# Attention and two expert layers on one core: third pair's weights in a buffer of their own, first product between the last steps, packed weights' casts ahead of their differences

## The chip, the cores and the metric

The kernel runs on one core of one Trainium2 chip. The metric is the device time of one execution in microseconds (us), as the median over runs. A core has engines that run side by side, each through its own list of instructions in order: TensorE (PE, matrix products), VectorE (DVE), ScalarE (ACT), GpSimd (POOL), and SyncE (SP), which here issues the DMA transfers. An instruction that needs a result of another engine waits at the head of its list, and everything behind it waits too.

## The reference

All arrays are float32. Attention runs twice per batch of 8 and head of 8: 32 packed queries attend to 576 tokens, and the tokens attend to the packed result. Two expert layers follow over 4608 tokens of width 512.

```python
    p_packed = sm_attn(p, k, v)
    out = sm_attn(q, p_packed, p_packed)
...
    h = x @ w_in
    g = np.where(h > 0.0, h, alpha * (np.exp(np.minimum(h, 0.0)) - 1.0))
    return (g @ w_out).astype(np.float32)
...
    a = x @ w_a
    b = x @ w_b
    return (a * b @ w_out).astype(np.float32)
```

`w_in` is 512 x 2048, `w_a` and `w_b` are 512 x 1536.

## The kernel before

A float32 product is made of three products of a shorter type (fp32r): each factor is split into a high word, which ScalarE casts, and a low word, which VectorE gets as a difference (`split`, L81 to L83). So nearly every tile that TensorE reads was first touched by ScalarE, then by VectorE.

**First phase** (to about 801 us). Eight blocks, one per batch, of 32 steps each; a step is a half h of the batch's tokens and a tile f of the hidden width. `l1` (L446) makes the hidden tile h with six matmuls (L455). `act1` (L461) makes the activation: ScalarE relu and exponential (ge, L463 and L464), VectorE gf (L467), ScalarE cast gr (L469), VectorE difference gr (L471). `l2` (L474) makes twelve matmuls into four accumulators x2a (L477), two steps later, through the list `pend`; it reads the cast in its first matmuls and the difference in the others. After the 16 steps of a half `x2_out` (L485) copies the accumulators out (L494 on ScalarE, L495 on VectorE) and stores them to x2d in memory (L496).

Between the steps lie the attention of the next batch and the conversion of the second expert layer's weights. They are put into a list with a time (`put`, L516; two units are a step), and `run_until` (L519) writes them into the program when the steps have come to that time. From block 1 on, TensorE, VectorE and ScalarE run in the order in which the program is written; SyncE's order, and all of block 0, are set by the scheduler. In attention, `wp` (L373) multiplies the packed result by the first layer's weights, one chunk c of four at a time, and `wps` (L378) splits the two rows of banks of such a chunk into the ring buffers wr that `l1` reads. `o_hi` and `o_lo` (L705, L708) split the rows of the last weights and store them to od. `pT` (L107) is a transpose of the packed queries on TensorE, with a copy by VectorE.

**Second phase.** Six groups of tokens; for each, twelve pairs f of weight tiles. `l3` (L878) makes seven products of sums (six matmuls each, L868) in banks A, B and C for a pair, with the sums of weights in a tile e (1792 KB) and the sums of activations s (22 steps, `s_steps`, L797, from the four tiles x2f that `x_load`, L786, brings back from x2d). ScalarE copies A and C (p1, p5), VectorE makes u, v and w of them. `l4` (L910) multiplies the result by wo into the group's accumulators, nine matmuls per pair (L912). The first group's s steps, and the e tiles of pairs 0 and 1, are made or loaded inside block 7 of the first phase. All other e tiles of the first group are loaded by `e_load` (L781, issue L783), into two buffers that pairs share in turn, so a load waits for the pair two before it to be done. The tiles for pairs 9 and 11 (`E_LATER`) are still computed in the first group (`e_words`, L761, brings the raw words wl; `e_step`, L769, works in the one buffer "em"; L680 stores to ed). `o_load` (L856, issue L858) brings wo, twelve loads of 512 KB.

```python
        E_LATER = {9: 1, 11: 5}
...
            put(T7 + 42 + 0.9 * n, s_step, 0, n)
...
                acc = [bank2("acc", f"o{g}_{t}", TT) for t in range(TT)]
                for f in range(NF2):
                    c1[f], c2[f] = l3(g, f)
                    if f + 2 < NF2:
                        e_load(f + 2, g)
```

Of the kernel before, what the change touches and what calls it, by code (L numbers as in the profile page):

```python
# [20 lines left out]
P = 128  # L21
# [4 lines left out]
def program(tc, q, k, v, p, w_in, w_out, w_a, w_b, w_out2, out):  # L26
# [34 lines left out]
    with ctx:  # L61
# [316 lines left out]
        def wps(b, c, r):  # L378
            w = ring_r[st[b, "wp", c]][r]
            split(w[:, 0, :], w[:, 1, :], st[b, "wpp"][r])  # L380
            if r == 1:
                done.add(("wp", b, c))

        def attention(b, tokens=False):

# [5 lines left out]
            def at_times(k, load_q, pt, s1s, sm1, q, sm1bs, at, at5, p, ppt, s2s, wps_):  # L391
# [26 lines left out]
                for c, t in enumerate(wps_):  # L418
                    add(t, wp, c, takes=("wp", b, c))
                    add(t + 1, wps, c, 0)  # L420
                    add(t + 2 if tokens else t + 1, wps, c, 1, frees=("wp", b, c))

# [192 lines left out]
        for b in range(1, B):  # L615
            for t, fn, takes, frees in attention(b):
                late = t > 64
                if b == 1:
                    packed = {48: 58, 49: 59, 52: 62, 53: 63, 56: 66, 57: 67, 60: 73, 61: 74}
                    t = packed.get(t, t + 2.3 if late else 22 + 0.8 * max(t, 0))  # L620
                    late = t > 64
                put(2 * NF * 2 * (b - 1) + t, fn, chain=(b, late), takes=takes, frees=frees)
# [99 lines left out]
        for b in range(1, B - 1):  # L722
            t, f = 4 * NF * b, 2 * (b - 1)
            first = (A1, B1, O1) if f in E_IN_1 else ((11, 12, 15), (18, 19, 21), O1)
            for f_, times in ((f, first), (f + 1, (A2, B2, O2))):
                for kind, x in zip("abo", times):
                    put(t + x[0] - 16, w2_load, kind, f_)
                    for n, y in enumerate((*x, x[2] + 3)):
                        put(t + y, w2_step, kind, f_, n)
            for f_, x, y in ((f, 25, 26), (f + 1, 61, 67)):  # L730
                put(t + x, o_hi, f_)
# [100 lines left out]
        E_IN_7 = (3, 5, 7, 0, 1)  # L832
        E_LATER = {9: 1, 11: 5}
        assert sorted((*E_IN_1, *E_IN_7, *E_LATER)) == list(range(NF2))
# [8 lines left out]
        for n in range(NS):  # L843
            put(T7 + 42 + 0.9 * n, s_step, 0, n)
        m1_block(B - 1)
        while pend:
            run_pend()
        order.close()
        order.enter_context(tc.manual_schedule(engines={ET.PE}))
        ps_stack.close()  # L850
        m1_stack.close()
        p4 = ctx.enter_context(tc.tile_pool(name="p4", bufs=2, side="right", reuse_waits="tile"))
        ps2 = ctx.enter_context(tc.tile_pool(name="ps2", bufs=1, space=PSUM, reuse_waits="tile"))
        wo = {}

        def o_load(f):  # L856
            wo[f] = p4.tile([P, 2, 512], F32R, tag=f"wo{f}", name=f"wo{f}", bufs=1)
            nc.sync.dma_start(wo[f].bitcast(F32), od[f])  # L858

        def bank2(tag, name, bufs):  # L860
# [3 lines left out]
        def product(bank, f, i, first=True):  # L864
            n = 0
            for k in range(2):
                for wi, xi in ((0, 0), (0, 1), (1, 0)):
# [8 lines left out]
                    n += 1  # L876

        def l3(g, f):  # L878
            def tmp(tag):
# [6 lines left out]

            bA, bB, bC = (bank2(x, f"{x}{g}_{f}", n) for x, n in (("A", 2), ("B", 2), ("C", 1)))
            pA, pB, pC = (x[:, :HT] for x in (bA, bB, bC))
            p1, u, v, p5, w = (tmp(x) for x in ("p1", "u", "v", "p5", "w"))
            product(bA, f, 1)  # L890
            nc.scalar.copy(p1, pA)  # L891
# [28 lines left out]
        def out_rows(g, t, acc):  # L920
# [6 lines left out]
            nc.sync.dma_start(out[r0:r0 + P, :], o)  # L927

        with order:
            for g in range(NG):  # L930
                c1, c2 = {}, {}
                acc = [bank2("acc", f"o{g}_{t}", TT) for t in range(TT)]
                for f in range(NF2):
                    c1[f], c2[f] = l3(g, f)
                    if f + 2 < NF2:
                        e_load(f + 2, g)
                    if g == 0:
                        o_load(f)
                        for n, f0 in E_LATER.items():
                            if f == f0 - 1:  # L940
                                e_words(n, True)
                            if 0 <= f - f0 < 3:
                                for names in E_STEPS[2 * (f - f0):2 * (f - f0) + 2]:
                                    for name in names:
                                        e_step(n, name, p4, "em", 1)
                    if f:
                        for t in range(TT):
# [48 lines left out]
```

## Time and profile before

| | before |
|---|---|
| median of 3 runs | 1641.36 us (1640.78 to 1642.24) |
| profiled execution, its own time | 1641.99 us |
| its span | 1640.2 us |
| TensorE, VectorE, ScalarE busy | 96%, 62%, 44% |
| mean granted clock of TensorE | 0.979 of full speed |

The span runs from the first to the last instruction of the one profiled execution; the time has a little more around it. A timeline row gives the start, the duration and the engine, the line of the program, what is written from what (`out<-in`), and how often; in brackets stands the idle time of the engine just before, and what ended it. SPq is SyncE issuing a transfer.

### The profile page before, as it was taken

The page shows a single profiled execution, that of the slowest core. Times are in us where ns is not written, and L with a number is a line of the kernel's source. Part 1 is how long each engine was busy: PE and PEld are TensorE (multiplying, and loading weights), DVE is VectorE, ACT ScalarE, POOL GpSimd, SP SyncE. Part 2 cuts the span into 40 slices and gives each one's busy share as a digit, 9 for nine tenths or more (in the row PEclk, how much of TensorE's full clock was granted, in tenths as well). Part 3 has the DMA queues.
Part 4 walks back from the last instruction along what each step waited for, and adds up shares of the span by engine and source line. Part 5 has one row for each costly group of instructions (what it writes and reads, how often), then busy time and mean ns, then how long its engine had stood idle before and what let it go on. Part 6 is the DMA issues. An engine that isn't in the chain of part 4 may idle for free.

```text
span 1640.2 us, 27529 instructions
## 1 busy us (share of the span) xinstructions
PE 1568.5 (96%) x10824; PEld 1437.7 (88%) x10824; DVE 1024.9 (62%) x2180; ACT 724.4 (44%) x1633; POOL 93.6 (6%) x74
## 2 busy tenths in 40 slices
PE   5498999999999999999899999999999999999998
PEld 3286898989898998989889899999989989998997
DVE  6999576777777777767645544635545454563451
ACT  6576566667676767667422212312222221231221
POOL 3321010100000001000000000000000000000000
PEclk7599999999999999999999999999999999999999
DMA  8755344626272543327495545535545553553541
GB/s 253 186 155 131 106 108 108 170 54 188 69 197 82 147 127 104 112 106 264 177 369 184 202 149 215 212 136 180 203 143 212 192 199 148 194 208 109 202 179 39
DMA packets 215505, 267.34 MB, mean 163 GB/s; under 512 B 150224, under 2 KB 180944, under 8 KB 205520
## 3 DMA queue, kind: packets, MB, share of 16 engines
q1 hardware_dynamic: 215376, 265.59, 48.8%
q8 instruction: 85, 1.39, 0.3%
q14 instruction: 44, 0.36, 0.1%
HBM read 213.52 MB, written 52.04 MB: 162 GB/s over the span
## 4 chain that ended last, share of the span: by engine, by line
PE 73%; DVE 11%; ACT 8%; DMA 4%; issue 2%; SPq 1%; POOL 0%; DVEq 0%; ACTq 0%
PE o L912 18%; PE x2a L477 16%; PE B L868 13%; PE A L868 9%; PE C L868 8%; PE h L455 8%; DVE gf L467 2%; DVE wr L83 2%; ACT gr L469 2%; ACT wr L82 2%; ACT ge L464 1%; DMA wst_i<-in_moe_w_in_dram 1%; ACT ge L463 1%; DVE gr L471 1%; DVE s L83 1%
## 5 line engine op out<-in xcount | busy, mean ns | idle before, releaser
L477 PE MATMUL x2a<-gr,wout 128*128 128x288 f32 x3072 | 464.7, 299 | 7.8 <-DVE x2s L495 2.4
L477 PEld LDWEIGHTS x2a<-gr,wout 128*128 128x128 f32 x3072 | 422.1, 189 | 51.6 <-issue 12.8
L912 PE MATMUL o<-wo,c 128*128 128x512 f32 x1296 | 307.7, 391 | 0.0
L912 PEld LDWEIGHTS o<-wo,c 128*128 128x128 f32 x1296 | 242.5, 188 | 47.8
L455 PE MATMUL h<-a,wr 128*128 128x288 f32 x1536 | 250.8, 299 | 17.0 <-DVE gf L467 9.4
L868 PE MATMUL B<-s,e 128*128 128x384 f32 x1296 | 261.3, 336 | 2.4 <-DVE u L893 1.0
L455 PEld LDWEIGHTS h<-a,wr 128*128 128x128 f32 x1536 | 220.9, 191 | 24.1 <-DVE gf L467 11.7
L868 PEld LDWEIGHTS B<-s,e 128*128 128x128 f32 x1296 | 228.2, 188 | 4.5 <-DVE v L898 2.4
L868 PE MATMUL A<-s,e 128*128 128x384 f32 x864 | 176.0, 338 | 5.5 <-DMA e<-ed 5.5
L868 PE MATMUL C<-s,e 128*128 128x384 f32 x864 | 173.9, 335 | 0.0
L868 PEld LDWEIGHTS A<-s,e 128*128 128x128 f32 x864 | 154.7, 189 | 12.0 <-DMA e<-ed 6.3
L469 ACT CAST gr<-gf 128x288 fp32r<-128x288 f32 x256 | 110.7, 433 | 121.3 <-DVE gf L467 120.1
L868 PEld LDWEIGHTS C<-s,e 128*128 128x128 f32 x864 | 152.7, 189 | 0.0
L82 ACT CAST c<-u 128x384 fp32r<-128x384 f32 x72 | 36.9, 513 | 259.2 <-DVE u L901 259.2
L467 DVE SCALAR_TENSOR_TENSOR gf<-ge,h 128x288 f32<-128x288 f32 x256 | 113.4, 443 | 58.1 <-ACT ge L464 54.7
L898 DVE TENSOR_TENSOR v<-p,B 128x384 f32<-128x384 f32 x72 | 39.8, 553 | 162.8 <-PE B L868 162.8
L471 DVE TENSOR_TENSOR gr<-gf,gr 128x288 fp32r<-128x288 f32 x256 | 124.1, 485 | 20.0 <-ACT gr L469 18.3
L463 ACT ACTIVATE ge<-h 128x288 f32<-128x288 f32 x256 | 104.6, 409 | 58.2 <-PE h L455 57.4
L464 ACT ACTIVATE ge<-ge 128x288 f32<-128x288 f32 x256 | 113.8, 445 | 7.6
L893 DVE TENSOR_TENSOR u<-p,B 128x384 f32<-128x384 f32 x72 | 39.8, 553 | 117.5 <-PE B L868 117.5
L891 ACT COPY p<-A 128x384 f32<-128x384 f32 x72 | 34.7, 482 | 136.7 <-PE A L868 136.7
L895 ACT COPY p<-C 128x384 f32<-128x384 f32 x72 | 34.7, 482 | 109.7 <-PE C L868 109.7
(357 smaller groups left out, 1398.1 us busy)
## 6 DMA issues: line engine op xcount, KB each, us to landing
e<-ed SPq DMA_DIRECT2D x70, 1792.0 KB, 7.2
ed<-e SPq DMA_DIRECT2D x7, 1792.0 KB, 6.7
x2d<-x2s SPq DMA_DIRECT2D x32, 288.0 KB, 2.7
out_dram<-osb SPq DMA_DIRECT2D x36, 256.0 KB, 2.0
v<-in_v_dram SPq DMA_DIRECT2D x8, 1024.0 KB, 6.8
wst_i<-in_moe_w_in_dram SPq DMA_DIRECT2D x16, 512.0 KB, 5.7
wst_o<-in_moe_w_out_dram SPq DMA_DIRECT2D x16, 512.0 KB, 4.9
kst<-in_k_dram SPq DMA_DIRECT2D x112, 72.0 KB, 2.6
```

The source lines that it names most:

```text
L82: nc.scalar.copy(hi, src)
L83: nc.vector.tensor_tensor(lo, src, hi.bitcast(F32), op=ALU.subtract)
L455: nc.tensor.matmul(t[:, :HS], w[:, wi, o * P:(o + 1) * P], x[:, xi, :], start=(n == 0), stop=(n == 5))
L463: nc.scalar.activation(e, t[:, :HS], AF.Relu, scale=-1.0)
L464: nc.scalar.activation(e, e, AF.Exp, scale=-1.0)
L467: nc.vector.scalar_tensor_tensor(g, e, -1.0, t[:, :HS], op0=ALU.add, op1=ALU.max)
L469: nc.scalar.copy(gr[:, 0, :], g)
L471: nc.vector.tensor_tensor(gr[:, 1, :], g, gr[:, 0, :].bitcast(F32), op=ALU.subtract)
L477: nc.tensor.matmul(acc[d][:, :HS], wout_r[f][:, wi, d * P:(d + 1) * P], gr[:, xi, :], start=(first and n == 0), stop=(last and n == 2),)
L868: nc.tensor.matmul(bank[:, :HT], es[f][:, E_OF[i], wi, k * P:(k + 1) * P], ss[i][:, xi, k, :], start=(first and n == 0), stop=(n == 5), sk ...
L893: nc.vector.tensor_tensor(u, p1, pB, op=ALU.add)
L912: nc.tensor.matmul(acc, cr[:, xi, t * P:(t + 1) * P], wo[f][:, wi, :], start=(f == 0 and n == 0), stop=(f == NF2 - 1 and n == 2),)
```

## The change

1. The split of the packed weights (blocks 1 to 7) is written as two functions: `wps_hi` makes both casts, `wps_lo` both differences, the latter one unit of time later than the casts.
2. For batch 1 the table `packed`, which sets the times of wp and its splits in block 0 and the first steps of block 1, gets other times. wp_1 comes ahead of x2a of h_1_8's step, wp_2 directly behind the transpose pTp at the end of block 0, wp_3 one step later than before, behind h_0_5.
3. `o_lo` of the second weight row of a block goes from 67 to 65.
4. `E_LATER` goes from {9: 1, 11: 5} to {9: 3, 11: 6}.
5. The s steps go from 42 + 0.9 n to 40.5 + 0.85 n.
6. The first product A of the second phase, before split in two lots of three matmuls among the steps of block 7, is written with all six between the last two `l2` of the first phase.
7. The e tile of pair 2 gets a buffer of its own ("em", shared with the tiles of pairs 9 and 11 afterwards), and its load is written ahead of the second phase; the loads for pairs 3 and 4 are written one pair earlier.
8. The accumulators of a group are allocated at pair 1 and no more at its start.

```diff
+        def wps_hi(b, c):
+            for r in range(2):
+                nc.scalar.copy(ring_r[st[b, "wp", c]][r][:, 0, :], st[b, "wpp"][r])
+
+        def wps_lo(b, c):
+            for r in range(2):
+                w = ring_r[st[b, "wp", c]][r]
+                nc.vector.tensor_tensor(w[:, 1, :], st[b, "wpp"][r], w[:, 0, :].bitcast(F32), op=ALU.subtract)
+            done.add(("wp", b, c))
...
-                    add(t + 1, wps, c, 0)
-                    add(t + 2 if tokens else t + 1, wps, c, 1, frees=("wp", b, c))
+                    if tokens:
+                        add(t + 1, wps, c, 0)
+                        add(t + 2, wps, c, 1, frees=("wp", b, c))
+                    else:
+                        add(t + 1, wps_hi, c)
+                        add(t + 2, wps_lo, c, frees=("wp", b, c))
...
-                    packed = {48: 58, 49: 59, 52: 62, 53: 63, 56: 66, 57: 67, 60: 73, 61: 74}
+                    packed = {
+                        48: 58, 49: 59, 50: 60, 52: 62, 53: 63, 54: 63.5, 56: 64.5, 57: 65, 58: 66, 60: 74.5, 61: 75, 62: 77
+                    }
...
-            for f_, x, y in ((f, 25, 26), (f + 1, 61, 67)):
+            for f_, x, y in ((f, 25, 26), (f + 1, 61, 65)):
...
-        E_LATER = {9: 1, 11: 5}
+        E_LATER = {9: 3, 11: 6}
...
-            put(T7 + 42 + 0.9 * n, s_step, 0, n)
+            put(T7 + 40.5 + 0.85 * n, s_step, 0, n)
...
-        while pend:
-            run_pend()
+        run_pend()
+        first_a = [bank2("A", "A0_0", 2)]
+        product(first_a[0], 0, 1)
+        run_pend()
+        assert not pend
...
+            started = bool(first_a)
+            bA = first_a.pop() if started else bank2("A", f"A{g}_{f}", 2)
...
+            if not started:
+                product(bA, f, 1)
...
+        es[2] = p4.tile([P, 7, 2, 2 * P], F32R, tag="em", name="e2_0_2", bufs=1)
+        nc.sync.dma_start(es[2].bitcast(F32), ed[2])
...
-                acc = [bank2("acc", f"o{g}_{t}", TT) for t in range(TT)]
...
-                    if f + 2 < NF2:
+                    if f + 2 < NF2 and (g or f > 2):
                         e_load(f + 2, g)
                     if g == 0:
+                        if f < 2:
+                            e_load(f + 3, g)
...
+                    if f == 1:
+                        acc = [bank2("acc", f"o{g}_{t}", TT) for t in range(TT)]
```

**VectorE at the start of a block** (here block 4; blocks 2 to 6 have the same). gf and gr are the activation's steps, wst_2o is the difference of `o_lo`, a the result of attention, x2s the copies of the finished accumulators. Before:

```order
L467 SCALAR_TENSOR_TENSOR gf_0_0_5829<-ge_0_0_5813,h_0_0_5806 128x288
L471 TENSOR_TENSOR gr_0_0_5831<-gf_0_0_5829,gr_0_0_5831 128x288
L467 SCALAR_TENSOR_TENSOR gf_0_1_5856<-ge_0_1_5853,h_0_1_5846 128x288
L367 TENSOR_TENSOR a_4_1_0_5860<-t_5096,a_4_1_0_5860 128x288
L710 TENSOR_TENSOR wst_2o_5359<-wm_2o_5644,wst_2o_5359 128x512
L471 TENSOR_TENSOR gr_0_1_5858<-gf_0_1_5856,gr_0_1_5858 128x288
L495 COPY x2s_1_0_0_5878<-x2a_1_0_1_5325 128x288
L495 COPY x2s_1_2_0_5882<-x2a_1_0_3_5327 128x288
```

With the change:

```order
L481 SCALAR_TENSOR_TENSOR gf_0_0_5829<-ge_0_0_5813,h_0_0_5806 128x288
L726 TENSOR_TENSOR wst_2o_5359<-wm_2o_5644,wst_2o_5359 128x512
L485 TENSOR_TENSOR gr_0_0_5831<-gf_0_0_5829,gr_0_0_5831 128x288
L481 SCALAR_TENSOR_TENSOR gf_0_1_5858<-ge_0_1_5855,h_0_1_5848 128x288
L367 TENSOR_TENSOR a_4_1_0_5862<-t_5096,a_4_1_0_5862 128x288
L485 TENSOR_TENSOR gr_0_1_5860<-gf_0_1_5858,gr_0_1_5860 128x288
L509 COPY x2s_1_0_0_5878<-x2a_1_0_1_5325 128x288
L509 COPY x2s_1_2_0_5882<-x2a_1_0_3_5327 128x288
```

The difference of `o_lo` moved from behind a to ahead of the first step's gr; what follows it up to the two copies stands one place earlier.

**TensorE at the end of the first phase.** A_0 is the first product of the second phase, x2a are the accumulators of the last half, gr_1_14 and gr_1_15 the activations of its last two steps. Before:

```order
L868 MATMUL A_0_10624<-s_0_10247,e_0_9999 128x384 x3
L455 MATMUL h_1_7_10304<-a_7_1_0_9524,wr_0_107 128x288 x3
L455 MATMUL h_1_7_10304<-a_7_1_1_9529,wr_1_108 128x288 x3
L477 MATMUL x2a_1_0_0_10160<-gr_1_5_10258,wout_88 128x288
L868 MATMUL A_0_10624<-s_0_10247,e_0_9999 128x384 x3
...
L477 MATMUL x2a_1_0_3_10163<-gr_1_14_10533,wout_97 128x288 x3
L477 MATMUL x2a_1_0_0_10160<-gr_1_15_10562,wout_98 128x288 x3
...
L477 MATMUL x2a_1_0_3_10163<-gr_1_15_10562,wout_98 128x288 x3
L868 MATMUL B_0_10625<-s_0_10249,e_0_9999 128x384 x6
```

With the change:

```order
L491 MATMUL x2a_1_0_3_10163<-gr_1_14_10535,wout_97 128x288 x3
L869 MATMUL A_0_10589<-s_0_10224,e_0_9999 128x384 x6
L491 MATMUL x2a_1_0_0_10160<-gr_1_15_10562,wout_98 128x288 x3
...
L491 MATMUL x2a_1_0_3_10163<-gr_1_15_10562,wout_98 128x288 x3
L869 MATMUL B_0_10630<-s_0_10226,e_0_9999 128x384 x6
L869 MATMUL C_0_10631<-s_0_10225,e_0_9999 128x384 x6
L869 MATMUL A_0_10589<-s_0_10228,e_0_9999 128x384 x6
```

The product A_0 moved from the steps around h_1_7 to between the products of gr_1_14 and those of gr_1_15.

**SyncE at the border of the phases.** x2d are the last two stores of the first phase; wo, wl and e_0_2 as above; ed_158 is the store of pair 9's computed tile. Before:

```order
L496 DMA x2d_1_124<-x2s_1_0_0_10601 128x576
L496 DMA x2d_1_124<-x2s_1_2_0_10605 128x576
L858 DMA wo_10691<-od_161 128x1024
L766 DMA wl_10693<-wfb_146 128x512
...
L858 DMA wo_11260<-od_168 128x1024
L766 DMA wl_11014<-wfa_136 128x512
L766 DMA wl_11014<-wfb_148 128x512
L858 DMA wo_11342<-od_169 128x1024
L783 DMA e_0_2_10689<-ed_151 128x3584
L858 DMA wo_11420<-od_170 128x1024
...
L680 DMA ed_158<-e_9_10765 128x3584
L783 DMA e_0_3_10761<-ed_152 128x3584
```

With the change:

```order
L510 DMA x2d_1_124<-x2s_1_0_0_10608 128x576
L510 DMA x2d_1_124<-x2s_1_2_0_10612 128x576
L952 DMA e_0_2_10628<-ed_151 128x3584
L895 DMA wo_10690<-od_161 128x1024
...
L895 DMA wo_11420<-od_170 128x1024
L799 DMA e_0_3_10688<-ed_152 128x3584
L895 DMA wo_11496<-od_171 128x1024
L895 DMA wo_11584<-od_172 128x1024
L782 DMA wl_11092<-wfa_136 128x512
L799 DMA e_0_4_10757<-ed_153 128x3584
L782 DMA wl_11092<-wfb_148 128x512
```

The load of e_0_2 moved to directly behind the two stores, e_0_3 and e_0_4 moved ahead of the store of pair 9.

## Rows read from the trace of the kernel before

**Rows 1.** The page, busy time by engine: us, share, instructions.

```profile
PE 1568.5 (96%) x10824; PEld 1437.7 (88%) x10824; DVE 1024.9 (62%) x2180; ACT 724.4 (44%) x1633; POOL 93.6 (6%) x74
```

**Rows 2.** TensorE's waits, 200 to 797 us: total us, times, longest.

```profile
PE x2a L477 <- DVE x2s L495: 2.4, 5, 0.5
PE x2a L477 <- ACT x2s L494: 1.3, 2, 0.9
...
PE x2a L477 <- DVE gr L471: 0.3, 1, 0.3
```

**Rows 3.** The same from 797 us to the end.

```profile
PE A L868 <- DMA e<-ed: 5.5, 1, 5.5
PE B L868 <- DVE u L893: 1.0, 1, 1.0
PE x2a L477 <- DVE gr L471: 1.0, 1, 1.0
```

**Rows 4.** Timelines of TensorE and VectorE, blocks 0 and 1.

```profile
183.56 0.72 PE L242 MATMUL s__2143<-kT,pT 64*32 64x288 f32 x16 [0.95 <-DVE wr L83]
...
199.26 0.92 PE L455 MATMUL h<-a,wr 128*128 128x288 f32 x5 [1.53 <-DVE gf L467]
...
197.49 0.69 DVE L83 TENSOR_TENSOR wr<-wp__2242,wr 128x512 fp32r<-128x512 f32 x1 [0.65 <-ACT wr L82]
```

**Rows 5.** Timelines of VectorE and TensorE, start of block 4.

```profile
452.77 0.46 DVE L471 TENSOR_TENSOR gr<-gf,gr 128x288 fp32r<-128x288 f32 x1 [0.50 <-ACT gr L469]
...
455.22 0.68 DVE L710 TENSOR_TENSOR wst_2o<-wm_2o,wst_2o 128x512 fp32r<-128x512 f32 x1
...
456.19 0.81 DVE L495 COPY x2s<-x2a 128x288 f32<-128x288 f32 x2
...
456.70 1.07 PE L477 MATMUL x2a<-gr,wout 128*128 128x288 f32 x6 [0.48 <-DVE x2s L495]
```

**Rows 6.** Chain of waits, end of the first phase: start, us, what.

```profile
768.55 4.01 DMA x2f<-x2d
...
797.11 0.46 DVE gr L471
...
797.62 3.35 PE x2a L477 x23
```

**Rows 7.** TensorE's timeline, end of the first phase and first pairs.

```profile
772.96 0.68 PE L868 MATMUL A<-s,e 128*128 128x384 f32 x3
...
796.24 0.40 PE L477 MATMUL x2a<-gr,wout 128*128 128x288 f32 x1 [0.36 <-ACT gr L469]
...
801.50 1.31 PE L868 MATMUL B<-s,e 128*128 128x384 f32 x6 [0.55 <-DVE x2s L495]
802.66 1.20 PE L868 MATMUL C<-s,e 128*128 128x384 f32 x6
803.70 1.20 PE L868 MATMUL A<-s,e 128*128 128x384 f32 x6
...
824.17 2.29 PE L868 MATMUL A<-s,e 128*128 128x384 f32 x6 [5.49 <-DMA e<-ed]
...
855.47 1.23 PE L868 MATMUL A<-s,e 128*128 128x384 f32 x6
...
864.87 1.23 PE L868 MATMUL A<-s,e 128*128 128x384 f32 x6
```

**Rows 8.** SyncE's timeline at the border, and the page's DMA issues (KB each, us to landing).

```profile
801.93 0.56 SPq L858 DMA_DIRECT2D wo<-od  x1
...
e<-ed SPq DMA_DIRECT2D x70, 1792.0 KB, 7.2
```

**Rows 9.** Table by stretch: busy us per engine, granted clock, DMA share, GB/s.

```profile
802.00:808.00 6.00, 6.00 (x36) 6.00 (x35) 1.75 (x4) 0.53 (x2) 0.00 (x0) 1.00 0.92 300
...
824.00:830.00 6.00, 5.83 (x18) 5.83 (x19) 0.56 (x1) 0.48 (x1) 0.00 (x0) 0.50 1.04 431
...
840.00:850.00 10.00, 10.00 (x56) 9.60 (x56) 6.52 (x13) 2.47 (x5) 0.00 (x0) 1.00 1.01 417
```

More of the change, by code (lines that the diff above doesn't have):

```diff
@@ L843, in program @@
         for n in range(NS):
-            put(T7 + 42 + 0.9 * n, s_step, 0, n)
-        m1_block(B - 1)
-        while pend:
-            run_pend()
[L848 to L858, printed above, removed]
+            put(T7 + 40.5 + 0.85 * n, s_step, 0, n)
         def bank2(tag, name, bufs):
@@ L876, in product, with o_load @@
                     n += 1
+        m1_block(B - 1)
+        run_pend()
[3 more added lines that the diff above has]
+        assert not pend
+        order.close()
+        order.enter_context(tc.manual_schedule(engines={ET.PE}))
+        ps_stack.close()
+        m1_stack.close()
+        p4 = ctx.enter_context(tc.tile_pool(name="p4", bufs=2, side="right", reuse_waits="tile"))
+        ps2 = ctx.enter_context(tc.tile_pool(name="ps2", bufs=1, space=PSUM, reuse_waits="tile"))
+        wo = {}
+        def o_load(f):
+            wo[f] = p4.tile([P, 2, 512], F32R, tag=f"wo{f}", name=f"wo{f}", bufs=1)
+            nc.sync.dma_start(wo[f].bitcast(F32), od[f])
         def l3(g, f):
@@ L885, in halves @@
                 return r
-            bA, bB, bC = (bank2(x, f"{x}{g}_{f}", n) for x, n in (("A", 2), ("B", 2), ("C", 1)))
+            started = bool(first_a)
+            bA = first_a.pop() if started else bank2("A", f"A{g}_{f}", 2)
+            bB, bC = (bank2(x, f"{x}{g}_{f}", n) for x, n in (("B", 2), ("C", 1)))
             pA, pB, pC = (x[:, :HT] for x in (bA, bB, bC))
             p1, u, v, p5, w = (tmp(x) for x in ("p1", "u", "v", "p5", "w"))
-            product(bA, f, 1)
+            if not started:
+                product(bA, f, 1)
             nc.scalar.copy(p1, pA)
```

## The prediction

> **What bounds the kernel now.** I read the page's busy times first: TensorE is busy 96% of the span [rows 1], so only TensorE's own waits can be won back, and work of other engines counts only where TensorE stands for it. The list of TensorE's waits comes next, in two stretches. From 200 to 797 us, in the first phase, five waits for a VectorE copy of a finished accumulator make 2.4 us, two for a ScalarE copy 1.3, one for a difference 0.3 [rows 2]. From 797 us on, one wait for the weights of a pair is 5.5 us and two of 1.0 stand beside it [rows 3]. The timelines then show what the waited-for engine did just before [rows 4, 5]; the chain of waits shows what held the end of the first phase [rows 6]; TensorE's and SyncE's timelines and the table by stretch show the border [rows 7 to 9]. The sum is made against the profiled execution, 1641.99 us (span 1640.2), 0.63 above the median of 1641.36; I take its difference over to the median.
>
> I call t0 the end of the first phase's last x2a product: 797.62 + 3.35 = 800.97 in the kernel before [rows 6].
>
> **Blocks 0 and 1.** TensorE waits 0.95 us for the second difference of wp_2 ahead of s, and 1.53 us for a gf that stands behind the differences of wp_3 [rows 4]. VectorE itself waits 0.65 between the two wp_3 differences, for ScalarE's next cast: that is the alternation which casts first, differences later, removes. wp_3 now goes behind gf_0_6, and wp_2 right behind the transpose pTp, whose copy it must then wait for. Nothing is removed from VectorE, so between -1.53 and 0 for the first I take -1.0 (the wait's cause, the two differences, leaves that gf's place whole, but lands ahead of gr_0_6), and between -0.95 and +0.5 for the second -0.5. wp_1's earlier place I cost at nothing: TensorE there waits for VectorE anyway. **-1.5** (bounds -2.5 to +0.5).
>
> **Five block boundaries.** Each boundary of blocks 1 to 6 has VectorE idle 0.50 us ahead of gr_0_0, and one step later a difference of o_lo (0.68) ahead of gr_0_1 and the two copies that TensorE waits for, 0.48 us [rows 5]. The o_lo difference goes into the idle place: gr_0_0 is 0.2 late, covered by the lag of two steps between gr and its x2a; the copies come 0.6 earlier, more than the 0.48. Its store to od and the load of pn pass each other on SyncE; od is read in the second phase only. 5 x 0.48 = **-2.4** (bounds -2.4 to 0). **Block 6 to 7**: the waits of 0.3 and 0.9 [rows 2] follow the alternation of wp_3's casts and differences. Now both differences stand behind gr_1_14, and o_lo leaves the block's first steps. I take the 0.3 and a third of the 0.9: **-0.6** (bounds -1.2 to 0).
>
> **End of the first phase.** The s steps cannot begin before x2f lands at 772.56; from there ScalarE and VectorE alternate, step after step, up to the difference of gr_1_14 at 797.11 [rows 6]. Starting the steps earlier in the order moves none of the 22 ahead of that landing in time worth naming, so the difference of gr_1_14 stays near 797.57. The first product's six matmuls stood at 772.96 and 1.5 us later, 0.68 each in two lots, with no wait ahead [rows 7]; there they only used time in which TensorE runs ahead of ScalarE and VectorE. Behind gr_1_14 they cost their 1.04 (six matmuls at the products' spacing) unless they fill a wait. The waits in question are 0.36 and 0.98 [rows 7, 3]; the s steps now end two activation steps before the end, so some of them goes: I take a third of the 1.34. t0 moves by +1.04 - 0.44 = **+0.6** (bounds -0.3 and +1.04).
>
> **After t0.** Before, the third pair's weights e_0_2 were issued behind nine wo and three wl, and landed as A_2 started, 824.17, after 5.49 of idle; the clock was at 0.50, that is 1.2 GHz, from 824 to 830, so six us of work at half speed cost some 2.9 more [rows 7 to 9]. Now e_0_2 is issued where the first wo was, 801.93, and a load of e lands 7.2 later [rows 8]: 809.1, t0 + 8.2. It is needed at t0 + 16.2: from B at 801.50 to A at 824.17 are 22.67, less the waits of 5.49 and 0.99 [rows 7, 3]. So that wait goes, with the half clock; the 0.55 ahead of B goes too, as B and C no longer take the banks that the x2s copies still read. I take u's 0.99 as gone, since VectorE has no s steps left to finish.
>
> But the queue carries all else as before, at 417 GB/s when full [rows 9]. Sizes are from the order's shapes at 4 bytes: 1.835 MB for e or a store to ed, 0.524 for wo, 0.262 for wl, 1.573 for the eight x2f. Behind e_0_2 stand ten wo, one wl, then e_0_3: 7.34 MB, 17.6 us, landing at 826.7, t0 + 25.8. Pairs are 9.4 apart (855.47 to 864.87 [rows 7]), so A_3 is due at t0 + 25.6: a wait of 0.2. From there to e_0_6 stand two wo, two wl, e_0_4, ed_9, e_0_5, x2f, ed_11 and e_0_6: 12.32 MB, 29.5 us, landing at t0 + 55.3, while A_6 is due at t0 + 54.0: **a new wait of some 1.3 us at the seventh pair**. e_0_4 and e_0_5 come in time. A_6 then starts at t0 + 55.3 instead of 864.87 - 800.97 = 63.9: **-8.6** (bounds -10.1 with no wait, -7 with 1.6 us more in the queue's start or a drop of clock behind the new wait). The steps of e_9 and e_11, later now, lie on ScalarE and VectorE; their results are first read for the tenth and twelfth pairs, 45 us after the stores. From A_6 on nothing differs.
>
> On that rate a page differs: the Trainium skill, DMA: Bandwidth & Descriptors, section "Where 436 GB/s comes from", holds that loads from HBM bind at some 358 GB/s per core. The trace shows 417 over ten us [rows 9], so the measurement decides; by 358 the sum would come to -4.0 in place of -12.5.
>
> **Sum**: -1.5 - 2.4 - 0.6 + 0.6 - 8.6 = **-12.5 us**: the profiled execution 1629.5, the median **1628.9**.
>
> **Rivals.**
> (a) *All waits go.* The queue keeps up and A_6 starts at t0 + 53.8 (-10.1); t0 moves by -0.3, blocks 0 and 1 give -2.5, block 6 to 7 -1.2, the boundaries -2.4: -16.5, 1624.9. For it: 1.3 us is little against 55; against: the count of bytes, and VectorE's load in block 0.
> (b) *The queue is slower.* Between 802 and 808, with the queue not yet full, it moved 300 GB/s [rows 9]. From 801.93 to e_0_6 there are 21.5 MB behind 2.8 us of start-up. At 358 GB/s, midway between 300 and 417, e_0_6 lands at t0 + 63.8, and only -4.0 is left: 1637.4; at 380, 1633.9. For it: e_0_2 now leads, and SyncE issues with gaps; against: 431 and 417 in the later stretches [rows 9]. The rule of the Trainium skill's DMA page, above, would bring this case.
> (c) *The early load is not early.* The buffer of its own shares memory with the first phase's tiles; if its load still waits until the first pair is done (six products, t0 + 6.2), e_0_2 is in time, but all that SyncE holds behind it comes 5.3 later: A_6 at t0 + 60.6, -3.3, sum -7.2: 1634.2. For it: the pool opens over released memory; against: those weights were last read long before t0.
> (d) *Slower.* The same queue, if the 300 GB/s of its first six us lasted up to e_0_6: 71.7 us for the bytes, A_6 at t0 + 75.4, +11.5, sum +7.6: 1649.0. With the other terms at -3.9 the change loses below 336 GB/s, and by over 0.2% below 319. Neither later stretch is near that.
>
> **How the numbers follow.** What a measurement of this kernel can tell from no change is some 0.2%, 3.3 us. The forecast has 0.55 (1626.5 to 1632), (a) 0.18, (b) 0.12, (c) 0.08, (d) 0.03, and 0.04 that two terms of the first phase turn into losses and little is left. The range 1624.5 to 1635.5 takes in (a), (c) and (b) down to 370 GB/s; left out are the rest of (b), (d), the 0.04 and a little below (a). Faster than 1638.1: all but (d) and most of the last, 0.92; the same 0.05; slower 0.03.
>
> **What would show it.** In the waits: the five for the x2s copies gone, gf's 1.53 gone, no wait for e at A_2 and a clock of 1.00 from t0 on; a short wait for e at A_3, and one of 1 to 2 us at A_6; x2a still waiting near 797, t0 within a us of 801.6. Wrong would be: a wait at A_2; a wait over 3 us at A_3 (then (b) or (c), told apart by when e_0_2 is issued); half clock behind a new wait; a new wait at pT or gr_0_6 in block 1 as long as those removed; t0 later than 802.

## The result and the profile after

| | before | after |
|---|---|---|
| median of 3 runs | 1641.36 us | 1626.11 us (1625.30 to 1629.78) |
| ratio, 95% interval | | 0.9912 (0.9888 to 0.9937) |
| timed again, median | 1644.00 us (7 runs) | 1629.74 us (4 runs), 0.9914 (0.9899 to 0.9929) |
| profiled execution, its own time | 1641.99 us | 1629.78 us |
| its span | 1640.2 us | 1628.0 us |
| forecast | | 1628.9 us (1624.5 to 1635.5) |

The kernel is faster by some 15 us (0.9%) in the first timing and 14 in the second; the forecast was 12.5. Sum and sign were right. The parts were not: two gains were far too small, two too large, one loss too small, and they nearly cancelled. That the sum came out is luck.

TensorE's waits in the profile after, from 150 to 200 us, from 200 to 797 and from 797 on (three lists; total us, times, longest). Hold them beside [rows 2, 3, 4]:

```profile
PE wp__1930 L242 <- DVE t L340: 2.4, 1, 2.4
PE x2a L491 <- DVE gr L485: 0.5, 1, 0.5
PE wp__2066 L242 <- DVE pT L111: 0.4, 1, 0.4
...
PE aTp L283 <- DVE wr L391: 2.8, 1, 2.8
PE x2a L491 <- DVE gr L485: 1.9, 5, 0.5
PE x2a L491 <- ACT x2s L508: 0.4, 1, 0.4
...
PE A L869 <- DMA e<-ed: 3.0, 2, 2.2
PE B L869 <- DVE v L920: 0.9, 5, 0.2
```

A_n is the first product of pair n in the first group. Gone are the five waits for VectorE's x2s copies, gf's 1.53, the 0.95 ahead of s, u's 0.99 and the 5.49 ahead of A_2. New are 2.8 us of a transpose aTp in block 1, 0.4 of wp for the copy pT, five waits for a difference gr in the second half of block 7, and two for the e tiles of later pairs.

TensorE's timeline after, end of the first phase and the first pairs, to hold beside [rows 7]:

```profile
786.64 1.75 PE L491 MATMUL x2a<-gr,wout 128*128 128x288 f32 x11 [0.47 <-DVE gr L485]
...
789.66 3.31 PE L491 MATMUL x2a<-gr,wout 128*128 128x288 f32 x23 [0.35 <-DVE gr L485]
792.81 1.21 PE L869 MATMUL A<-s,e 128*128 128x384 f32 x6
793.85 1.76 PE L491 MATMUL x2a<-gr,wout 128*128 128x288 f32 x12
795.45 1.21 PE L869 MATMUL B<-s,e 128*128 128x384 f32 x6
...
811.07 1.21 PE L869 MATMUL A<-s,e 128*128 128x384 f32 x6
...
822.75 1.31 PE L869 MATMUL A<-s,e 128*128 128x384 f32 x6 [2.16 <-DMA e<-ed]
...
852.48 1.34 PE L869 MATMUL A<-s,e 128*128 128x384 f32 x6 [0.86 <-DMA e<-ed]
```

B starts behind the last x2a without a wait, A_2 (811.07) behind the first o products without one, A_3 waits 2.16 and A_6 0.86. A_0 stands whole at 792.81, and TensorE had work on both sides of it: no idle time is shown behind 789.66.

To see where the time went I cut each profiled execution at the same products in TensorE's timeline: the first h of block 2, of block 7 and of block 7's second half (its 17th step), the first B behind the last x2a, and A_8, behind which the first group runs without waits. Lengths in us:

| profile | start to block 2 | blocks 2 to 6 | block 7, first half | second half, to B | B to A_8 | A_8 to the end |
|---|---|---|---|---|---|---|
| before | 269.56 | 446.13 | 39.93 | 45.88 | 82.16 | 756.52 |
| after | 272.26 | 438.19 | 38.23 | 46.76 | 75.94 | 756.59 |
| after, timed again | 271.98 | 438.21 | 38.19 | 47.38 | 76.06 | 756.60 |
| difference of the first two | +2.70 | -7.94 | -1.70 | +0.88 | -6.22 | +0.07 |

The stretches behind the start of block 2 give -14.9 us, about what the medians say; the profiled execution lost 2.7 of it ahead of block 2. Of that 1.06 is block 1; 2.14 lie ahead of the 17th step of block 0, a stretch that differs as much between profiles of the same code there (last section).

### The profile page after: what moved, and what is told of

The parts are those of the page before. It is cut to its first block, busy times and chain, and to the rows that moved or that the text cites. A ratio compares the mean times of both kernels' runs of the same rounds, so it can differ in the third digit from the quotient of the medians.

```text
span 1628.0 us, 27573 instructions
## 1 busy us (share of the span) xinstructions
PE 1564.8 (96%) x10824; PEld 1438.3 (88%) x10824; DVE 1025.0 (63%) x2180; ACT 722.6 (44%) x1633; POOL 93.8 (6%) x74
## 4 chain that ended last, share of the span: by engine, by line
PE 84%; DVE 7%; DMA 4%; ACT 3%; issue 1%; SPq 1%; POOL 0%; DVEq 0%; ACTq 0%
PE x2a L491 22%; PE o L934 18%; PE B L869 12%; PE h L469 11%; PE A L869 8%; PE C L869 8%; DMA e<-ed 2%; DMA x2f<-x2d 1%; DVE s L83 1%; DMA wl<-wfb 1%; DMA wst_i<-in_moe_w_in_dram 1%; SPq L166 1%; PE pp L303 1%; DVE wout L151 0%; DVE gf L481 0%
```

## The experiments

All kernels stand in this table, cut at the same places; the text below takes them one by one. "Time" is the median, of one execution where no interval was taken. The first four are the kernel before with one part of the change; it took 1642.92 beside them, 1643.09 beside the next four (the changed kernel with one part set otherwise), and 1644.00 beside the last three.

| run | time | to block 2 | blocks 2 to 6 | block 7, first half | second half, to B | B to A_8 | to the end |
|---|---|---|---|---|---|---|---|
| split order alone | 1635.68 | 271.13 | 440.11 | 38.23 | 45.91 | 81.89 | 756.61 |
| o_lo alone | 1642.69 | 273.07 | 442.75 | 39.90 | 46.18 | 82.47 | 756.54 |
| batch 1 alone | 1646.18 | 272.67 | 445.97 | 39.93 | 45.87 | 83.38 | 756.56 |
| border loads alone | 1636.55 | 271.00 | 445.82 | 39.92 | 45.30 | 76.12 | 756.61 |
| A_0 in the waits | 1626.85 | 270.38 | 438.19 | 38.23 | 45.77 | 75.89 | 756.59 |
| s steps later | 1628.60 | 271.45 | 438.25 | 38.19 | 46.03 | 76.37 | 756.51 |
| wp_3 earlier | 1627.34 | 267.17 | 438.21 | 38.19 | 48.32 | 77.04 | 756.61 |
| loads by need | 1631.88 | 271.63 | 438.21 | 38.23 | 46.82 | 73.63 | 761.59 |
| change again | 1629.74 | 271.98 | 438.21 | 38.19 | 47.38 | 76.06 | 756.60 |
| three parts mended | 1625.09 | 269.14 | 438.19 | 38.23 | 45.07 | 76.04 | 756.62 |
| and loads by need for six pairs | 1621.83 | 267.44 | 438.19 | 38.19 | 45.00 | 73.48 | 756.71 |

**Split order alone.**

```diff
-                    add(t + 1, wps, c, 0)
-                    add(t + 2 if tokens else t + 1, wps, c, 1, frees=("wp", b, c))
+                    if tokens or b == 1:
+                        add(t + 1, wps, c, 0)
+                        add(t + 2 if tokens else t + 1, wps, c, 1, frees=("wp", b, c))
+                    else:
+                        add(t + 1, wps_hi, c)
+                        add(t + 2, wps_lo, c, frees=("wp", b, c))
```

`wps_hi` and `wps_lo` are the two functions of the change.

> The kernel before, with casts first and differences later for the packed weights of blocks 2 to 7 alone. Theory A: the two differences end some 2 us earlier, the bank pair of the packed weights comes free, and the transpose pTp at each block's start no longer stands for it; the five waits of pTp (0.9 us in the list, 0.3 to 0.5 more hidden in the gap ahead of each) go, 0.5 to 1.0 us per block from block 2 to 7: -3 to -6 us between the starts of blocks 2 and the end of block 7, with o_lo's wait of 0.48 at each boundary still there. Theory B, the prediction's: only block 6 to 7 has a wait of this kind, -0.3 to -0.6, and the boundaries stay as they were.

Blocks 2 to 6 are 6.02 us shorter, block 7's first half 1.70: theory A, and more than its 3 to 6. How it comes about is seen at the start of block 4. VectorE's and TensorE's timelines of the kernel before:

```profile
447.10 0.69 DVE L83 TENSOR_TENSOR wr<-wp__5746,wr 128x512 fp32r<-128x512 f32 x1 [0.99 <-ACT wr L82]
448.44 0.69 DVE L83 TENSOR_TENSOR wr<-wp__5746,wr 128x512 fp32r<-128x512 f32 x1 [0.65 <-ACT wr L82]
...
448.12 0.95 PE L455 MATMUL h<-a,wr 128*128 128x288 f32 x6
449.24 0.30 PE L109 MATMUL pTp<-ident,pn 128*128 128x128 f32 x1 [0.16 <-PE h L455]
449.29 2.02 PE L477 MATMUL x2a<-gr,wout 128*128 128x288 f32 x12
```

and of this run:

```profile
445.41 1.29 DVE L391 TENSOR_TENSOR wr<-wp__5746,wr 128x512 fp32r<-128x512 f32 x2 [0.52 <-ACT wr L386]
...
447.24 0.96 PE L469 MATMUL h<-a,wr 128*128 128x288 f32 x6
448.05 0.27 PE L109 MATMUL pTp<-ident,pn 128*128 128x128 f32 x1
448.07 1.87 PE L491 MATMUL x2a<-gr,wout 128*128 128x288 f32 x12
```

Before, VectorE stood 0.99 and 0.65 for ScalarE's casts, and the second difference ended at 449.13; pTp, which takes the pair of banks that this difference reads, started at 449.24, 1.12 behind the start of h. Now both differences run back to back, end by 446.7, and pTp starts 0.81 behind h's start. The list gives pTp's wait to h, but behind h alone pTp can start 0.81 after h's start, as this run shows: the engine named had been done, and the difference was what came last. VectorE is also ahead later on: VectorE's five copies x2s are no longer waited for, and of ScalarE's two one of 0.4 is left, though o_lo stands where it stood. From one start of h to the next, block 4 lost 0.48 at its first step (pTp), 0.51 at its third (the copies) and 0.13 at its 31st, of 1.28 in all.

**o_lo alone.**

```diff
-            for f_, x, y in ((f, 25, 26), (f + 1, 61, 67)):
+            for f_, x, y in ((f, 25, 26), (f + 1, 61, 65)):
```

> The kernel before, with o_lo of the second row at 65 in place of 67 alone. Theory A and the prediction: the five waits of x2a for the x2s copies, 0.48 each, go: -2.4 us between the starts of blocks 2 and 7; pTp's waits stay. Rival: the copies still come late because gf and gr ahead of them wait for ScalarE, and 0 to -1 is left.

Blocks 2 to 6 are 3.38 us shorter, not 2.4: 0.68 a block, 0.6 of it at the copies, where the wait shown was 0.48. The waits for VectorE's x2s are gone and pTp's stay, as the waits of this run from 280 to 797 us show:

```profile
PE x2a L477 <- ACT x2s L494: 1.3, 2, 1.0
PE pTp L109 <- PE h L455: 0.7, 4, 0.2
```

The two parts overlap: -6.02 and -3.38 alone, -7.94 together, since both help the copies: the third step of block 4 lost 0.51 with the one, 0.60 with the other and 0.84 with both. The run's whole time hardly differs from before (1642.69 to 1642.92), as its stretch to block 2 was 3.5 us longer in instructions that are the same up to there; more on that below.

**Batch 1 alone.** The table `packed` and the split order of batch 1 as in the change, all else as before.

```diff
-                    packed = {48: 58, 49: 59, 52: 62, 53: 63, 56: 66, 57: 67, 60: 73, 61: 74}
+                    packed = {48: 58, 49: 59, 50: 60, 52: 62, 53: 63, 54: 63.5, 56: 64.5, 57: 65, 58: 66, 60: 74.5, 61: 75, 62: 77}
```

> The kernel before, with the new times and the new split order for the packed weights of batch 1 alone (block 0 and the first steps of block 1). Prediction: -1.5 us by the start of block 2. Theory A, after the profile of the changed kernel: a wait of some 2.8 us of a transpose aTp for the differences of wp_3, in place of the 1.53 of h for gf, so that block 1 is 0.5 to 1.5 us longer than before, and block 0's second half 0.3 to 0.6 shorter; the sum is 0 to +1 at the start of block 2.

Block 1, from its first h to that of block 2, takes 95.23 us, 94.05 before and 95.11 after the change: this part makes block 1 longer by 1.1 to 1.2, and the prediction's -1.5 falls. The wait is in the waits of this run as in the changed kernel:

```profile
PE aTp L283 <- DVE wr L391: 2.8, 1, 2.8
```

VectorE's and TensorE's timelines of the changed kernel show how it comes:

```profile
200.44 0.46 DVE L481 SCALAR_TENSOR_TENSOR gf<-ge,h 128x288 f32<-128x288 f32 x1 [0.45 <-ACT ge L478]
200.82 1.28 DVE L391 TENSOR_TENSOR wr<-wp__2275,wr 128x512 fp32r<-128x512 f32 x2
...
202.24 1.24 PE L283 MATMUL aTp<-ident,e 128*128 128x128 f32 x8 [2.77 <-DVE wr L391]
```

The differences of wp_3 stand behind gf_0_6, and gf_0_6 waits for ScalarE. aTp takes the bank pair that these differences read, and it is due 2.77 us before they end. What block 0 gains is small: its second half took 51.5 to 51.6 in three of the four profiles with the old times there and 52.8 in the fourth; with the new times it took 50.3 to 51.4 in all eight profiles of the changed kernel and its variants, but 52.7 in this run. Some -0.6 is likely. So the expected sum of 0 to +1 at the start of block 2 is not seen in this one execution (+3.1).

**Border loads alone.** The load of e_0_2 into "em", e_0_3 and e_0_4 one pair earlier, `E_LATER` and the allocation at pair 1, all as in the diff of the change; A_0 and the s steps as before.

> The kernel before, with the early load of the third pair's weights, the loads of pairs 3 and 4 one pair earlier, the later steps of pairs 9 and 11 and the later allocation of the accumulators; A_0 stays in two lots among the steps, the s steps stay. Theory A: the time from the last x2a of the first phase to A_6, 64.2 us before and 57.2 in the changed kernel, is 56 to 58; a wait for e of 1.5 to 2.5 at A_3 and of 0.5 to 1.5 at A_6, none at A_2; the first phase is as before, so that the whole is 6 to 8 us shorter than before. Rival: without the moved A_0 the first product after the border starts no earlier and a wait for the copies or for u comes back: 4 to 5 us.

From B to A_8 76.12 us, 75.94 in the change and 82.16 before: the border's gain is this part's alone, -6.0, and 0.6 more ahead of B, where the wait for the x2s copies (0.55) is gone. From B to A_6 are 57.2, with 3.2 us of waits for e at two pairs (longest 2.2): theory A. The four parts of this run (the early load, the two loads a pair earlier, the later steps, the later allocation) were not taken apart.

**A_0 in the waits.** In the changed kernel, three matmuls behind h_1_14 and three behind h_1_15, each ahead of an x2a that waited (0.47 and 0.35).

```diff
-        run_pend()
-        first_a = [bank2("A", "A0_0", 2)]
-        product(first_a[0], 0, 1)
-        run_pend()
+        first_a = [bank2("A", "A0_0", 2)]
+        put(T7 + 60.5, product, first_a[0], 0, 1, True, (0,))
+        put(T7 + 62.5, product, first_a[0], 0, 1, True, (1,))
+        m1_block(B - 1)
+        while pend:
+            run_pend()
```

> The changed kernel, but the first product A_0 in two lots of three matmuls again, behind h_1_14 and behind h_1_15, ahead of the x2a that waited 0.47 and 0.35 us for a difference. Theory A: where it stands in the change it costs its whole 1.04, since TensorE has all its last work ready there; in the waits it costs 0.2, so from the 17th step of block 7 to the last x2a it is 45.7 us in place of 46.6, and the end is 0.6 to 1.0 earlier against that step. Theory B: the change's place fills a wait, and the lots cost as much in the new place: 0.

From the 17th step to B 45.77 in place of 46.76: -0.99, theory A. The six matmuls cost next to nothing in these places. TensorE's timeline of this run has no wait left behind 780:

```profile
783.98 0.69 PE L869 MATMUL A<-s,e 128*128 128x384 f32 x3
784.51 2.00 PE L491 MATMUL x2a<-gr,wout 128*128 128x288 f32 x12
786.34 0.96 PE L469 MATMUL h<-a,wr 128*128 128x288 f32 x6
787.14 0.68 PE L869 MATMUL A<-s,e 128*128 128x384 f32 x3
787.66 5.07 PE L491 MATMUL x2a<-gr,wout 128*128 128x288 f32 x36
```

So the move of A_0 to between the last steps, as the change has it, loses nearly its whole 1.04 against these places. The stretch depends on the landing of x2f too (below, at wp_3 earlier), but that came alike: 17.59 us behind the 17th step here, 17.56 in the change.

**s steps later.** The changed kernel with the old times of these steps.

```diff
-            put(T7 + 40.5 + 0.85 * n, s_step, 0, n)
+            put(T7 + 42 + 0.9 * n, s_step, 0, n)
```

> The changed kernel with the s steps at the times of before (42 + 0.9 n). Theory A: the steps are gated by the landing of x2f in both orders; with the later times the wait ahead of the last x2a products falls two steps later, at gr_1_14, and A_0 then fills part of 0.98, so that the stretch from the 17th step of block 7 to the last x2a is within 0.5 us of the changed kernel's 46.6, rather shorter. Theory B, the change's aim: the earlier steps let the last activations come sooner, and with the later ones the stretch is 1 to 2 us longer.

From the 17th step to B 46.03, 0.73 shorter: theory A's direction, by more than its 0.5. The earlier steps only put ScalarE and VectorE in front of x2f's landing sooner. Behind that landing (17.45 us after the 17th step) TensorE's waits are then those of before, 0.36 and 0.98 at gr_1_14, and one of 0.38 at gr_1_11; A_0 stands behind them.

**wp_3 earlier.** The changed kernel with the two differences of wp_3 behind gr_0_5.

```diff
-                        48: 58, 49: 59, 50: 60, 52: 62, 53: 63, 54: 63.5, 56: 64.5, 57: 65, 58: 66, 60: 74.5, 61: 75, 62: 77
+                        48: 58, 49: 59, 50: 60, 52: 62, 53: 63, 54: 63.5, 56: 64.5, 57: 65, 58: 66, 60: 74.5, 61: 75, 62: 76
```

> The changed kernel with the two differences of batch 1's last packed weights one unit of time earlier (76 in place of 77), behind gr_0_5 and ahead of gf_0_6. Theory A: aTp waits for these differences, as it takes the bank pair that they still read; one place earlier in VectorE's order takes 1 to 2 us off the wait of 2.77, the clock drop behind it stays away, and block 1 is 1.5 to 2.5 us shorter than in the changed kernel. Rival: VectorE is full there, the wait moves to gf_0_6 and h (0.8 or more), and block 1 is within 0.7 us.

Block 1 takes 91.62 us: 3.5 less than in the change and 2.4 less than before, more than theory A had. aTp's wait in TensorE's timeline:

```profile
198.39 1.21 PE L283 MATMUL aTp<-ident,e 128*128 128x128 f32 x8 [0.50 <-DVE nm L273]
```

In the same profile the end of block 7 was 1.56 longer than in the change. Its x2f load took 5.75 us in the chain of waits (4.23 in the change's), and TensorE stood 1.81 for the first difference behind the landing; nothing in block 7's own code differs. With the s steps early, an x2f that lands late goes straight through to TensorE: in the four profiles with this code in block 7 it landed 17.56 us (the change), 17.60 (loads by need), 18.13 (the change again) and 19.09 (this run) behind the 17th step, and the stretch from there to B took 46.76, 46.82, 47.38 and 48.32.

**Loads by need.** The changed kernel with SyncE in the program's order from the border on, and wo written two pairs ahead of its use.

```diff
-        order.enter_context(tc.manual_schedule(engines={ET.PE}))
+        order.enter_context(tc.manual_schedule(engines={ET.PE, ET.SP}))
...
+        for f in range(2):
+            o_load(f)
...
-                        o_load(f)
+                        if f + 2 < NF2:
+                            o_load(f + 2)
```

> The changed kernel with SyncE in the order of the program from the border on, and wo written two pairs ahead of its use: then e_0_3 stands behind two wo and not behind ten and one wl, and x2f behind all e loads of the first group. Theory A: the waits for e at A_3 (2.2) and A_6 (0.9) are the queue's, so both go; from the last x2a to A_6 it is 53.8 to 54.5 us in place of 57.2: -2.7 to -3.4 at the end. Rival: SyncE now stands for each buffer in turn, and a wait for wo at the first o products or for a later e takes their place: within 1 us of the changed kernel, or longer.

B to A_8 is 73.63 us, 2.3 less, and B to A_6 53.48, 3.5 less: the waits at A_3 and A_6 were the queue's. But from A_8 on it loses 5.0 us. So its one execution is slower than the change's as a whole, and theory A holds up to A_7 alone. The waits from 797 us on show what came:

```profile
PE B L869 <- DVE v L920: 4.2, 5, 0.9
PE A L869 <- DMA e<-ed: 1.7, 1, 1.7
```

One of the five waits for v stands at pair 7 of the first group (0.84), four in later groups (0.64 to 0.91), whose loads SyncE now issues in the program's order too; v waited at most 0.2 in the change. The e of A_11 (1.65) was issued at 891.11, when the store of pair 11, in front of it in the program's order, had landed. Which of SyncE's later places makes v late was not taken apart.

**The change again**, with an interval.

> The changed kernel itself, timed again. 1625 to 1630 us, 13 to 16 us under the kernel before; in the profile the stages from the start of block 2 on as in the first profile (within 0.3 us each), while the start of block 1 lies where the run's first 150 us put it.

1629.74 us, 14.3 under the kernel before on that chip. The stages are as expected, but for the end of block 7 (0.62 longer, a wait of 0.82 behind the landing of x2f in place of 0.29).

**Three parts mended.** The old times of the s steps and 62: 76, as above, and A_0 ahead of the last two lots of x2a:

```diff
-        run_pend()
-        first_a = [bank2("A", "A0_0", 2)]
-        product(first_a[0], 0, 1)
-        run_pend()
+        first_a = [bank2("A", "A0_0", 2)]
+        product(first_a[0], 0, 1)
+        run_pend()
+        run_pend()
```

> The changed kernel with three of its parts set otherwise: the s steps as before (42 + 0.9 n), A_0 whole but ahead of the products of gr_1_14, where TensorE waited 1.34 us in all, and the differences of batch 1's last packed weights at 76. If the runs so far add up: -3.5 in block 1, -0.7 and -0.9 at the end of the first phase: some 5 us under the changed kernel, 1621 to 1622. Rival: the gain at the end of the phase is lost again to a longer wait for e at A_3, since the queue's end stays where the x2d stores put it, no: these move along; then what is lost is A_0's cost if gr_1_14 comes sooner, at most 0.9.

1625.09 us (1623.53 to 1626.66), 4.65 under the change on the same chip; 0.9885 of the kernel before (0.9870 to 0.9900). Block 1 takes 91.71, the end of block 7 45.07: -3.4 in block 1 and -1.7 there against the change's first profile, so they nearly add up. The 1621 to 1622 that were expected go with the first timing's 1626.11 for the change (1629.74 beside this run) and were missed. TensorE's timeline shows A_0 filling the wait:

```profile
785.52 1.23 PE L869 MATMUL A<-s,e 128*128 128x384 f32 x6
786.58 0.29 PE L491 MATMUL x2a<-gr,wout 128*128 128x288 f32 x1
787.46 3.34 PE L491 MATMUL x2a<-gr,wout 128*128 128x288 f32 x23 [0.58 <-DVE gr L485]
```

**And loads by need, for six pairs.** The same, and SyncE as in loads by need up to pair 5 (wo written two pairs ahead), in the scheduler's order from there:

```diff
+                    if g == 0 and f == 6:
+                        order.close()
+                        order.enter_context(tc.manual_schedule(engines={ET.PE}))
```

> As the run before, and SyncE in the order of the program for the first six pairs alone, after them in the scheduler's: e_0_3 then stands behind six wo in place of ten wo and one wl, e_0_6 ahead of the store of pair 9 and of x2f. The waits for e at A_3 and A_6 (2.2 and 0.9) go and nothing comes for them, since the later groups keep their order: 2.5 to 3.2 us under the run before, 1618 to 1619.5. Rival: the wait moves to a later e of the first group, as where SyncE was in the program's order throughout (A_8 and A_11): 0 to 1.5 us under it.

1621.83 us (1620.80 to 1624.28), 7.9 under the change and 22 under the kernel before: 0.9870 (0.9854 to 0.9887). B to A_8 is 73.48 and the later groups are as before (756.71), so the part that cost 5 us is left out. SyncE's timeline has e_0_3 issued behind six wo at 797.05, 8.2 us after B's start at 788.82; in the change it was 809.36, 13.9 after. First this run, then the change:

```profile
789.20 0.38 SPq L952 DMA_DIRECT2D e<-ed  x1
...
790.12 3.07 SPq L895 DMA_DIRECT2D wo<-od  x6
797.05 0.32 SPq L799 DMA_DIRECT2D e<-ed  x1
...
796.58 0.70 SPq L952 DMA_DIRECT2D e<-ed  x1
...
809.36 0.33 SPq L799 DMA_DIRECT2D e<-ed  x1
```

One wait for e of 1.3 is left, at A_8, whose load was issued behind the store of pair 9: the rival in part. From B to A_8 it gains 2.56 on the run before, in the medians 3.3; the expected 1618 to 1619.5 was missed, as the run before lay above its own forecast. This version beats both kernels.

## Why the prediction was right in sum, point by point

**Blocks 0 and 1: -1.5 forecast; it failed.** The step was that the differences of wp_3 leave gf's place whole and land ahead of gr_0_6. They do, and gf's 1.53 is gone. What it left out is who else waits behind them: aTp needs their bank pair. Block 1 became 1.1 longer, with a wait of 2.77 and the clock at half behind it (below); with block 0's likely -0.6 that makes +0.5. One place earlier in VectorE's order the same part gives -2.4 in block 1.

**Boundaries of blocks 2 to 6: -2.4 forecast, -7.9 measured**, far outside the bounds. The o_lo term was mis-sized: 0.68 a boundary alone, in place of 0.48. The larger failure is that the split order was put at nothing here: it was priced only in blocks 0, 1 and 6 to 7. The rows of the kernel before had it: VectorE's 0.65 ahead of a second difference is in [rows 4] for wp_3 of batch 1, and the other blocks have such pairs too. I read past five waits of pTp, 0.9 us, because the list gave them to h. The split order alone is worth 6.0 in these blocks.

**Block 6 to 7: -0.6 forecast, -1.7 measured**, outside the bounds, all of it from the split order (the same 38.23 with that part alone). The waits of 0.3 and 0.9 were the right ones; I took a third of the second where the whole of it goes. The two steps of h that hold them shrank by 0.64 and 1.06, somewhat more than the waits shown.

**End of the first phase: +0.6 forecast, +1.6 measured** (from the 17th step to t0 46.92 in place of 45.35), outside the bounds. The reason was right, that A_0 was hidden where it stood and is not where it went; the step that a third of the 1.34 would be filled was wrong. So was that starting the s steps earlier moves nothing worth naming. x2f landed alike, 17.56 us behind the 17th step and 17.53 before, but with the earlier s steps TensorE's waits for gr fell at gr_1_5, 6, 10, 12 and 13 (1.9 in all), ahead of A_0's place. The run with A_0 in the waits puts 1.0 on A_0, the one with the s steps later 0.7 on these. The chain of waits of the changed kernel shows the end of it:

```profile
762.02 4.23 DMA x2f<-x2d
...
789.15 0.46 DVE gr L485
...
789.66 3.31 PE x2a L491 x23
792.97 1.04 PE A L869 x6
794.01 1.60 PE x2a L491 x12
```

**After t0: -8.6 forecast, -7.0 measured**, at the edge of the bounds. t0 is 794.01 + 1.60 = 795.61 now; A_6 starts at t0 + 56.9, where 55.3 was forecast and 63.9 stood before. The early load, the missing half clock and the waits that go were right: A_2 starts at t0 + 15.5, with the clock at 1.00. The term that was mis-sized is the queue's start. e_0_2 was issued when forecast, at t0 + 1.0, but took 8.2 us to land where the median of 7.2 was put in: t0 + 9.2 in place of 8.2. That is 1.0 of the 1.5 that A_6 came late, and the case of which the bound of -7 spoke. The rest was nearly as forecast: 17.95 us on to the landing of e_0_3 (17.6 forecast) and 29.72 on to that of e_0_6 (29.5). So A_3 waited 2.16 where 0.2 was forecast, as e_0_3 landed at t0 + 27.1 and not 25.8, and A_6 0.86 where 1.3 was, being due later itself. The table by stretch of the changed kernel (duration, busy time of each engine, granted clock, DMA share, GB/s):

```profile
796.00:802.00 6.00, 6.00 (x36) 6.00 (x35) 2.71 (x6) 0.61 (x2) 0.00 (x0) 1.00 0.93 343
802.00:812.00 10.00, 10.00 (x57) 9.60 (x56) 7.37 (x17) 2.54 (x6) 0.00 (x0) 1.00 1.00 403
812.00:822.00 10.00, 8.60 (x47) 7.85 (x45) 6.67 (x14) 4.12 (x9) 0.00 (x0) 1.00 1.02 419
...
842.00:852.00 10.00, 9.62 (x52) 8.82 (x51) 6.88 (x14) 1.99 (x4) 0.00 (x0) 1.00 1.00 398
```

The bytes behind e_0_2 (7.34 and 12.32 MB) moved at 409 GB/s up to e_0_3 and 414 up to e_0_6, so the 417 was right to 2%; the first six us had 343. The Trainium skill's 358 GB/s per core (DMA: Bandwidth & Descriptors, "Where 436 GB/s comes from") is not what binds here: the ten-us stretches show 398 and more.

**The rivals.** (a) fell with the waits at A_3 and A_6, though its 1624.9 is nearer to the median of 1626.11 than the forecast's 1628.9; (b) came in part, in the queue's start above all, with 1.3 us at e_0_3; (c) fell: A_2 waits for nothing; (d) had nothing for it.

**The sum.** Behind the start of block 2 the stretches came to -14.9 where -11.0 was forecast. Ahead of it -1.5 was forecast and block 1 was 1.1 longer. Three of the five terms lie outside their own bounds and the other two at the edge; that the sum lies 2.8 from the median is their cancelling.

## What to carry to other kernels

Where one engine's two instructions feed another's two, write both of the first ahead of both of the second: here the alternating pairs cost the second engine a wait each time (0.99 and 0.65), and whoever took the buffer next paid for it. Before a late step is moved, list everything that takes its buffers next, not only what stands behind it in its queue; a wait that is put down to an engine long done is the hint. Work without a waiter belongs into an existing wait of its engine, and loads onto a shared queue in the order in which they are needed, since all bytes ahead of a tile are part of its price.

## What I had not expected of the hardware

The stretch to block 2 differs by up to 3.5 us between executions of the same code: 269.56, 271.13, 271.00 and 273.07 in the four profiles that have the old code there (the second with the new split order for batch 2, late in block 1). Most of it lies ahead of the 17th step of block 0: 124.05, 125.64, 125.36 and 126.25. The five blocks behind repeat to 0.1 in the eight profiles with the change's code there, and to 0.3 in the three with the old. A gain of this size is read from the later stretches more surely than from three runs.

The clock falls behind a wait in one execution and not in the other. In the changed kernel the wait of 2.77 ahead of aTp was followed by a granted clock of 0.50, that is 1.2 GHz; the wait of 2.16 at A_3 was not. The first profile:

```profile
204.00:206.00 2.00, 2.00 (x10) 2.00 (x10) 1.21 (x3) 0.92 (x3) 1.02 (x1) 0.50 0.45 74
...
824.00:826.00 2.00, 2.00 (x14) 2.00 (x13) 0.55 (x1) 0.48 (x1) 0.00 (x0) 1.00 1.05 438
```

The same kernel timed again waited 2.28 at A_3, and there it fell:

```profile
824.00:826.00 2.00, 2.00 (x8) 1.98 (x8) 0.00 (x0) 0.48 (x1) 0.00 (x0) 0.53 1.02 424
826.00:828.00 2.00, 2.00 (x9) 2.00 (x9) 0.55 (x1) 0.00 (x0) 0.00 (x0) 0.61 1.06 452
```

Measured from B, A_4 came 1.7 us later than in the first profile, but A_6 only 0.3: there the e tile sets the time, and the wait for it swallowed the slower products.

The length of the wait alone does not tell. In all thirteen profiles a product wp in block 0 waits 2.2 to 2.8 us for a tile t; the clock fell to 0.50 with it in ten and stayed at 1.00 in three, with waits of 2.30 (before), 2.28 (wp_3 earlier) and 2.66 (the last run), while it fell with one of 2.24 (border loads alone). The wait of 2.77 ahead of aTp was followed by 0.50 in all six profiles that have it; at A_3 the clock stayed at 1.00 behind 2.16 to 2.25 in five profiles and fell behind 2.28 and 2.73.
